# A layer-norm, attention and gated-MLP kernel: the first query pair by seven products, and final adds from PSUM

## The chip, the cores and the metric

The kernel runs on one core of one Trainium2 chip. The metric is device time in microseconds, the median of several runs. Engines: TensorE (PE, and PEld for its weight loads), VectorE (DVE), ScalarE (ACT), GpSimd (POOL) and SyncE (SP), which issues nearly all DMAs. Each engine works through its own queue in program order and waits on semaphores.

## The reference, cut to what matters

```
xn = layernorm(x)                                  # x: 1 x 2048 x 512, bf16
q  = (xn @ wq) in 32 heads of 128
p  = softmax(q k^T / sqrt(128)); o = p v           # k_cache, v_cache: 32 heads, 2048 keys
s  = concat(o) @ wo
gate = xn @ W_gate; up = xn @ W_up                 # F = 1792
y  = (gate * (gate > 0) * up) @ W_down
out = x + s * silu(y)
```

## The kernel before, in words

The 2048 rows stand in four query blocks `Q` of 512 (16 tiles of 128 rows). All is one straight program; the order on each engine is the order in which the Python code emits.

**Start.** `head_ln` centres the rows of block 0 (`xc_sb`, transposed by TensorE into `xcT`). `emit_gate_up(0)` then runs the 14 chunks `fc` of 128 columns of gate and up for block 0 from these centred rows: 4 matmuls of gate, 4 of up, a ReLU on ScalarE into `gr_sb`, and a product `h` on VectorE (L620). Behind each chunk `ln_task(fc)` does a piece of the layer norm of the other rows: `ln_stats` of one tile, and once per block `ln_sqrt` on ScalarE, then `ln_finish(Q)`: coefficients on VectorE (`ln_coef`, L400, L403), four normalised tiles `xn_sb` on GpSimd (L409), and for each a DMA transpose into `xnT` issued by SP (L521). Blocks 1, 2, 3 come in this order at chunks 4, 8 and 12; SP then issues the first loads of keys, values and weights (`issue_first`), and block 0's own normalised tiles follow at chunk 13, with the factors `r2`, `r2h` of block 0's output.

`emit_down(0)` multiplies block 0's `h` with `W_down`: four tiles `j` of 14 matmuls into two banks of `ps_acc` in turn (L747). Each tile has a tanh on ScalarE (L755), and two operations on VectorE (L759, L763) that write `g_sb`; the tile after next waits for them. `emit_gate_up(2)` is the same as above for block 2, from `xnT`; into its chunks are put the scaling of `W_down` and its sums (`emit_wd_scale`, `emit_wd_sums`), row sums of `xnT` (`emit_tx`), sums of `h` (`emit_hs`) and `gu_sums`, the weight sums of one gate/up chunk of blocks 1 and 3 (scaling on ScalarE, four operations on GpSimd).

**Products.** Most later multiplications are done as 2 x 2 blocks by seven products instead of eight (Winograd's form): sums of weights (`emit_sw` for a pair of query heads, on GpSimd, into `SW`) and sums of rows (`emit_tx`, on VectorE, into `TX`, which lies over `xn_sb` and therefore waits until all sixteen transposes have read it), and the combination of the products on VectorE. For a pair `pr` of query heads that is `emit_st(pr, c, step)`, with `c` a half of the columns and four steps of two, two, two and one products, each of two matmuls. `emit_tx(k)` with `k = 4 c + i` makes the row sum `i` of half `c`. Pair 0 alone is projected directly by `emit_qp`: eight groups of four matmuls (L815).

**Attention.** 128 blocks `b` (head x query block), each of 8 pairs `p` of key tiles. For a pair: two score matmuls (L1258), one exponential on ScalarE (L1270), eight PV matmuls of 129 columns (L1367). Scores run `LAG` = 3 pairs ahead. Scores and all side products share three slots of two PSUM banks, in turn (`ring_acquire`): a slot is free when the work that read it last has ended. `emit_M(items)` takes a slot for side products. The table `plan` sets products at a `(b, p)`, `side` sets VectorE work there. At a block's end VectorE normalises (L1287, L1290), and the first PV matmul of the next block waits for this.

**End.** `emit_base` (L1235, L1240), by the list `base_at`, makes the part of the output that does not need the last four heads, two operations on VectorE for each tile. `emit_final_tile(n)` multiplies the last four heads' output with `wo` (four matmuls, L1401), scales by `g_sb` on VectorE into `fin_tmp` (L1409) and has GpSimd add (L1425), VectorE for the last tile alone; SP stores.

Of the kernel before, what the change touches and what calls it, by code (L numbers as in the profile page):

```python
# [52 lines left out]
def bass_recurrent_scan__mha_block_cached__glu_gated_reglu__prompt_kernel(  # L53
# [62 lines left out]
    with ExitStack() as es:  # L116
# [70 lines left out]
        cu = at_(92160, [128, NQ], F32, "cu")  # L187
        cv = at_(94208, [128, NQ], F32, "cv")
# [336 lines left out]
        def ln_task(i):  # L525
            if i < 4 * (QB - 1):
                ln_hold["st"] = ln_stats(4 + i)
                if i % 4 == 3:
                    ns = list(range(i + 1, i + 5))
                    ln_hold["sq"] = (ns, ln_sqrt(ns, ln_aggr(ns, ln_hold["st"])))  # L530
                elif i >= 4 and i % 4 == 0:
                    ln_finish(i // 4)
            elif i == 4 * (QB - 1):
                ln_finish(QB - 1)
                issue_first()
                ns = list(range(4))
                ln_hold["sq"] = (ns, ln_sqrt(ns, sem_ln2.cur()))
            elif i == 4 * (QB - 1) + 1:
                ctok = ln_finish(0)
                _wait(dve, ctok)  # L540
                rtok = sem_ln3.sig(
                    dve.scalar_tensor_tensor(r2[:], rstd[:, 0:4, :], YSC, rstd[:, 0:4, :],
                                             op0=ALU.mult, op1=ALU.mult))
                _wait(dve, rtok)
                ln_hold["r2"] = sem_ln3.sig(
                    dve.tensor_scalar(r2h[:], r2[:], 0.5 / YSC, None, op0=ALU.mult))
# [38 lines left out]
        def gu_sums(k):  # L585
# [13 lines left out]
            gu_tok[(k, "x")] = sem_sg.sig(pool.tensor_tensor(X[:, 3], a12, X[:, 1], ALU.subtract))  # L599

# [133 lines left out]
        def emit_down(Q, h_last_tok):  # L734
            assert Q == 0
            ytok = None
            for j in range(4):
# [28 lines left out]
                acc_free[jb] = gtok  # L766
            y_last["t"] = ytok
# [5 lines left out]
        _wait(sp, sem_g.cur())  # L773
        gu_load(0)
        gu_load(1)
        hlast = emit_gate_up(2)

        qt_ready = {}
        qp_done_tok = {}
# [28 lines left out]
        def emit_qp(h, Q, bank):  # L808
            qs = slice(Q * NQ, (Q + 1) * NQ)
            _wait(pe, wq_tok(0))  # L810
            if h == 0 and Q == 0:
                _wait_all(pe, xt_ready[0])
            ins = None
            for c in range(DC):
                ins = pe.matmul(ps_r[:, bank, :], Wq_sb[0][:, c, h, :], xnT[:, c, qs],  # L815
                                start=(c == 0), stop=(c == DC - 1))
            qtok = sem_qp.sig(ins)
            if h == 1 and Q == QB - 1:
                qp_done_tok[0] = qtok
            dst = qt_take(h, Q)  # L820
            if h == 0 and Q % 2 == 1:
                _wait(act, qtok)
                etok = sem_gua.sig(act.copy(dst, ps_r[:, bank, :]))
            else:
                _wait(dve, qtok)
                etok = sem_qpe.sig(dve.tensor_copy(dst, ps_r[:, bank, :]))
            qt_ready[(h, Q)] = etok
            return etok

        sw_tok = {}  # L830

        def emit_sw(pr):
            b = pr % 2
            W = Wq_sb[b]
            _wait(pool, wq_tok(pr))
            if pr >= 3:
                _wait(pool, qp_done_tok[pr - 2])
            wflat = W[:].rearrange("p c i e -> p (c i e)")
            if pr == 2:
                _wait(act, wq_tok(pr))  # L840
                k = sem_w2s.sig(act.activation(wflat, wflat, ACTF.Copy, scale=WSC))
            else:
                k = sem_sw.sig(pool.tensor_scalar(wflat, wflat, WSC, None, op0=ALU.mult))  # L843
            sw_tok[(pr, 0)] = k
            _wait(pool, k)
            a11, a12 = W[:, 0:HC, 0, :], W[:, HC:DC, 0, :]
            a21, a22 = W[:, 0:HC, 1, :], W[:, HC:DC, 1, :]
            X = SW[b]
            if pr == 1:
                _wait(pool, glu_done_tok)  # L850
            k1 = sem_sw.sig(pool.tensor_tensor(X[:, 0], a21, a22, ALU.add))
            sem_sw.sig(pool.tensor_tensor(X[:, 2], a11, a21, ALU.subtract))
            _wait(pool, k1)
            k2 = sem_sw.sig(pool.tensor_tensor(X[:, 1], X[:, 0], a11, ALU.subtract))
            _wait(pool, k2)
            sw_tok[(pr, 1)] = sem_sw.sig(pool.tensor_tensor(X[:, 3], a12, X[:, 1], ALU.subtract))

        st_tok = {}

        def emit_st(pr, c, step, *banks):  # L860
            W, X = Wq_sb[pr % 2], SW[pr % 2]
# [24 lines left out]
            if step == 0:  # L886
                _wait(pe, sw_tok[(pr, 0)])
                p1 = prod(1, banks[0])
# [365 lines left out]
        def emit_S_tile(gp, tt):  # L1254
# [8 lines left out]
            if p == NP - 1:  # L1263
                qt_free.append((qt_slot[(h, Q)], stok))
                if Q == QB - 1:
# [5 lines left out]
                               scale=scale if h < 2 else scale / WSC)  # L1271
# [119 lines left out]
        def emit_final_tile(n, bank):  # L1391
# [12 lines left out]
            fb = fin_cnt[0] % NFT  # L1404
            fin_cnt[0] += 1
            _wait(dve, otok)
            _wait(dve, fin_free[fb])
            mtok = sem_opa.sig(
                dve.scalar_tensor_tensor(fin_tmp[fb], ps_r[:, bank, 0:D], 1.0 / (OSC * YSC), g_sb[:, n, :],  # L1409
                                         op0=ALU.mult, op1=ALU.mult))  # L1410
            fin_pending.append((n, fb, mtok))
            flush_final_add()
            return mtok

        fin_pending = []

        def flush_final_add():
            if not fin_pending:
                return
            n, fb, mtok = fin_pending.pop()  # L1420
            Q, j = divmod(n, 4)
            eng, sem = (dve, sem_opa) if n == NT - 1 else (pool, sem_hp)
            _wait(eng, mtok)
            _wait(eng, base_done[n])
            ftok = sem.sig(eng.tensor_tensor(g_sb[:, n, :], s_acc[:, n, :], fin_tmp[fb], ALU.add))  # L1425
            fin_free[fb] = ftok
            if Q == QB - 1 or j % 2 == 1:
                n0 = n if Q == QB - 1 else n - 1
                _wait(sp, ftok)
                sem_out.sig(sp.dma_start(out_t[:, n0:n + 1, :], g_sb[:, n0:n + 1, :]))  # L1430

# [5 lines left out]
        at(0, 0, (emit_qp, 1, 1, 0), (emit_qp, 1, 1, 1))  # L1437
        at(1, 0, (emit_qp, 1, 1, 2), (emit_qp, 1, 1, 3))
# [29 lines left out]
        for i in range(4):  # L1468
            side.setdefault((i // 2, (6, 7)[i % 2] if i < 2 else (1, 3)[i % 2]), []).append((emit_tx, i))
# [28 lines left out]
        base_at += [(LB + 1, 6), (LB + 1, 7), (LB + 2, 2), (LB + 2, 6)]  # L1498
# [7 lines left out]

# [96 lines left out]
```

## Time and profile before

| | |
|---|---|
| median of 3 runs | 1255.91 us (1255.69 to 1256.41) |
| the profiled execution | 1255.73 us, of which the span 1254.1 |
| granted TensorE clock | 1.000 |
| busy share of the span: PE, DVE, ACT, POOL | 98%, 54%, 81%, 23% |

A timeline row gives the start, the length, the engine, the line, the operation, the tile written and the tiles read, and how often; in brackets, how long the engine stood idle before it and what released it. "SPq" is SP's issuing of a DMA, not the transfer. A matmul's length is that of its way through the array; the next starts earlier. A few matmul records are missing, so a count can be one or two short. A group row of the page has the busy time, the mean in ns, and the idle time before.

### The profile page before, as it was taken

The numbers are of one execution on the slowest core, as the hardware profiler recorded it, in microseconds if no ns is written. First come the engines' busy times: TensorE is split into PE (matmuls) and PEld (weight loads), VectorE is DVE, ScalarE is ACT, GpSimd is POOL, SyncE is SP. The second block draws the span as 40 slices with busy tenths as digits, with TensorE's granted clock in tenths as the row PEclk, the third lists the DMA queues.
The fourth block names the chain that finished last, engine by engine and source line by source line (L and its number), as shares of the span: only waits on it lengthen the run. The fifth ranks groups of instructions, "written<-read, shape, count | busy, mean of one in ns | idle before, by whom it ended". The sixth has DMA issues, their size and how long they took to land.

```text
span 1254.1 us, 28671 instructions
## 1 busy us (share of the span) xinstructions
PE 1234.5 (98%) x12173; PEld 868.8 (69%) x12399; DVE 681.7 (54%) x1157; ACT 1020.3 (81%) x1108; POOL 290.3 (23%) x261
## 2 busy tenths in 40 slices
PE   9999999999999999999999999999999999999998
PEld 5466565777777777777777777777777777777774
DVE  6667777665444545454543544454544444446766
ACT  4357877668888888888888888888888888888894
POOL 2323999510401040100401040102200040100005
PEclk9999999999999999999999999999999999999999
DMA  9712431332223332443222232433333222343212
GB/s 273 155 31 31 78 79 27 51 48 34 48 44 56 69 60 47 60 68 56 52 41 44 57 56 52 60 64 60 51 56 68 50 34 42 60 81 68 67 33 76
DMA packets 250687, 78.02 MB, mean 62 GB/s; under 512 B 226241, under 2 KB 250561, under 8 KB 250561
## 3 DMA queue, kind: packets, MB, share of 16 engines
q1 hardware_dynamic: 249888, 75.79, 32.6%
q8 instruction: 98, 1.61, 0.6%
q10 hardware_dynamic: 672, 0.39, 0.1%
q14 instruction: 29, 0.23, 0.1%
HBM read 38.54 MB, written 2.10 MB: 32 GB/s over the span
## 4 chain that ended last, share of the span: by engine, by line
PE 84%; ACT 10%; POOL 2%; issue 1%; SPq 1%; DVE 1%; DMA 0%; POOLq 0%; DVEq 0%; ACTq 0%
PE ps_acc L1367 34%; PE ps_r L1258 28%; ACT PT L1270 10%; PE ps_r L1139 6%; PE ps_r L879 6%; PE ps_r L943 3%; PE ps_r L1002 3%; PE ps_r L656 1%; PE ps_r L660 1%; PE ps_r L1401 1%; PE ps_r L815 1%; POOL hT L921 0%; SPq L521 0%; POOL xn_sb L409 0%; POOL gB L919 0%
## 5 line engine op out<-in xcount | busy, mean ns | idle before, releaser
L1270 ACT ACTIVATE PT<-ps_r 128x1024 bf16<-128x1024 f32 x1024 | 969.9, 1028 | 161.2 <-PE ps_r L1258 149.7
L1367 PE MATMUL ps_acc<-V_sb,PT 128*128 128x129 bf16 x8192 | 749.2, 220 | 10.0 <-DVE Onorm L1290 1.3
L1367 PEld LDWEIGHTS ps_acc<-V_sb,PT 128*128 128x128 bf16 x8192 | 605.0, 98 | 219.0 <-ACT PT L1270 16.0
L1258 PE MATMUL ps_r<-QT_sb,KT_sb 128*128 128x512 bf16 x1831 | 652.7, 379 | 2.0 <-ACT PT L1270 0.2
L1157 DVE TENSOR_TENSOR s_acc<-s_acc,ps_r 128x512 f32<-128x512 f32 x264 | 167.7, 683 | 178.1 <-PE ps_r L1139 178.1
L843 POOL TENSOR_SCALAR Wq_sb<-Wq_sb 128x1024 bf16<-128x1024 bf16 x14 | 38.8, 2771 | 675.9 <-DMA Wq_sb<-in_A_wq_dram 675.9
L1258 PEld LDWEIGHTS ps_r<-QT_sb,KT_sb 128*128 128x128 bf16 x2048 | 188.0, 98 | 1.6 <-ACT PT L1270 0.7
L1287 DVE RECIPROCAL rz_sb<-ps_acc 128x4 f32<-128x4 f32 x127 | 23.2, 183 | 204.1 <-PE ps_acc L1367 203.8
L1290 DVE TENSOR_TENSOR Onorm<-ps_acc,rz_sb 128x512 bf16<-128x512 f32 x127 | 87.8, 691 | 4.4
L884 DVE TENSOR_TENSOR QT_sb<-cu,ps_r 128x512 bf16<-128x512 f32 x60 | 41.3, 688 | 84.6 <-PE ps_r L1258 79.5
L1425 POOL TENSOR_TENSOR g_sb<-s_acc,WX 128x512 bf16<-128x512 f32 x15 | 17.8, 1216 | 153.9 <-DVE WX L1409 153.9
L879 PE MATMUL ps_r<-xn_sb,SW 128*128 128x512 f16 x180 | 48.6, 379 | 0.0
L1139 PE MATMUL ps_r<-WX,OX 128*128 128x256 f16 x336 | 45.8, 273 | 0.0
L884 DVE TENSOR_TENSOR cu<-cu,ps_r 128x512 f32<-128x512 f32 x60 | 41.3, 688 | 0.0
L1139 PEld LDWEIGHTS ps_r<-WX,OX 128*128 128x128 f16 x336 | 32.9, 98 | 9.8 <-ACT PT L1270 0.2
L884 DVE TENSOR_TENSOR QT_sb<-cv,ps_r 128x512 bf16<-128x512 f32 x60 | 38.3, 680 | 0.0
L1081 POOL TENSOR_SCALAR Wo_sb<-Wo_sb 128x2048 bf16<-128x2048 bf16 x7 | 37.6, 5366 | 0.6
L879 PEld LDWEIGHTS ps_r<-xn_sb,SW 128*128 128x128 f16 x180 | 17.6, 98 | 21.3 <-ACT PT L1270 0.3
L879 PE MATMUL ps_r<-xnT,Wq_sb 128*128 128x512 bf16 x120 | 30.8, 379 | 0.0
L1139 PE MATMUL ps_r<-Wo_sb,OT_store 128*128 128x256 bf16 x224 | 29.0, 273 | 0.4
L616 ACT ACTIVATE gr_sb<-ps_r 128x512 bf16<-128x512 f32 x27 | 15.7, 593 | 16.7 <-PE ps_r L656 16.0
L919 POOL TENSOR_SCALAR gB<-gB 128x512 bf16<-128x512 bf16 x14 | 20.8, 1487 | 32.2 <-DVE gB L949 32.2
(151 smaller groups left out, 942.4 us busy)
## 6 DMA issues: line engine op xcount, KB each, us to landing
V_sb<-in_A_v_cache_dram SPq DMA_DIRECT2D x32, 512.0 KB, 4.8
Wq_sb<-in_A_wq_dram SPq DMA_DIRECT2D x16, 256.0 KB, 3.8
Wo_sb<-in_A_wo_dram SPq DMA_DIRECT2D x8, 512.0 KB, 3.8
xr_sb<-in_A_x_dram SPq DMA_DIRECT2D x16, 128.0 KB, 2.1
OT_store<-Onorm SPq DMA_TRANSPOSE x127, 2.5
Wd_sb<-in_B_W_down_dram SPq DMA_DIRECT2D x1, 1792.0 KB, 14.0
W<-in_B_W_gate_dram SPq DMA_DIRECT2D x14, 128.0 KB, 2.5
W<-in_B_W_up_dram SPq DMA_DIRECT2D x14, 128.0 KB, 2.8
```

Source lines behind the costliest of these rows:

```text
L843: k = sem_sw.sig(pool.tensor_scalar(wflat, wflat, WSC, None, op0=ALU.mult))
L879: ins = pe.matmul(ps_r[:, bank, :], L(i), R(i), start=(i == 0), stop=(i == HC - 1))
L884: return sem_qpe.sig(dve.tensor_tensor(dst, a, ps_r[:, bank, :], op))
L943: ins = pe.matmul(ps_r[:, bank, :], L(i), R(i), start=(i == 0), stop=(i == HC - 1))
L1002: ins = pe.matmul(ps_r[:, bank, j * DH:(j + 1) * DH], L(i), R(i), start=(i == 0 and j == 0), stop=(i == HF - 1 and j == 1))
L1081: k = sem_wx.sig(pool.tensor_scalar(wflat, wflat, WOSC, None, op0=ALU.mult))
L1139: ins = pe.matmul(ps_r[:, bank, j * DH:(j + 1) * DH], L(i), R(i), start=(i == 0 and j == 0), stop=(i == GH - 1 and j == 1))
L1157: t = dve.tensor_tensor(names[k], names[k], view(bank), op)
L1258: ins = pe.matmul(ps_r[:, 2 * s + tt, :], KT_sb[h % 2][:, t * 128:(t + 1) * 128], QT_sb[qt_slot[(h, Q)]][:], start=True, stop=True)
L1270: act.activation(PT[pb][:], ps_r[:, 2 * s:2 * s + 2, :], ACTF.Exp, scale=scale if h < 2 else scale / WSC)
L1290: dve.tensor_tensor(Onorm[ob][:], o_ap, rz_sb[:].to_broadcast([128, 4, Dh]), ALU.mult))
L1367: ins = pe.matmul(o_ap, PT[pb][:, tt, j * 128:(j + 1) * 128], V_sb[vb][:, t, 0:VW], start=(t == 0 and j % 2 == 0), stop=(t == KT - 1 and j ...
```

## The change

- Block 0's normalised rows come first: the square root at chunk 1, `ln_finish(0)`, `r2` and `r2h` at chunk 2 of the first gate/up.
- The eight row sums `emit_tx` move into `emit_down`, two behind each tile's `g_sb`.
- Pair 0 goes by seven products: `emit_sw(0)` (scaling on ScalarE) behind chunk 0 of `emit_gate_up(2)`, the steps of the first half behind chunks 9 to 12, step 0 of the second half behind chunk 13, and its other three in attention blocks 0 and 1. `gu_sums` moves from chunks 4 and 6 to 7 and 9, `emit_hs` from 10 and 11 to 12 and 13. The combinations of the first half use buffers of their own (`cuv0`, `SW0`).
- The first three score pairs (`emit_S_pair`) stand behind chunks 12 and 13 instead of after them.
- Tiles 0 to 7, 10, 13 and 15 of the end are scaled in place in PSUM and added by VectorE; the others stay with GpSimd.
- The last four entries of `base_at` move to later pairs.

```diff
@@ ln_task
+                if i == 1:
+                    ns = list(range(4))
+                    ln_hold["sq"] = (ns, ln_sqrt(ns, sem_ln2.cur()))
                 ln_hold["st"] = ln_stats(4 + i)
+                if i == 2:
+                    ctok = ln_finish(0)
...
@@ emit_sw
-            if pr == 2:
+            if pr in (0, 2):
                 _wait(act, wq_tok(pr))
...
@@ emit_gate_up, Q == 2
-                    elif fc < 10:
-                        emit_tx(fc - 2)
-                    elif fc < 12:
-                        emit_hs(2, 0, 2 * (fc - 10))
-                        emit_hs(2, 0, 2 * (fc - 10) + 1)
-                    if fc in (4, 6):
-                        gu_sums(fc // 2 - 2)
+                    if fc == 0:
+                        emit_sw(0)
+                    if fc in (7, 9):
+                        gu_sums((fc - 7) // 2)
+                    if 9 <= fc < 12:
+                        emit_M([(emit_st, 2, 0, 0, fc - 9)])
+                    elif fc == 12:
+                        emit_S_pair(0)
+                        emit_M([(emit_st, 1, 0, 0, 3)])
+                    elif fc == 13:
+                        emit_S_pair(1)
+                        emit_M([(emit_st, 2, 0, 1, 0)])
+                        emit_S_pair(2)
+                    if fc > 11:
+                        emit_hs(2, 0, 2 * (fc - 12))
+                        emit_hs(2, 0, 2 * (fc - 12) + 1)
@@ emit_down, end of tile j
                 acc_free[jb] = gtok
+                emit_tx(2 * j)
+                emit_tx(2 * j + 1)
@@ emit_final_tile
+            sums_on_dve = n < NT - 8 or n in (NT - 6, NT - 3, NT - 1)
...
+            if sums_on_dve:
+                eng, sem, prod = dve, sem_opa, ps_r[:, bank, 0:D]
+            else:
+                eng, sem = pool, sem_hp
...
@@ plan and main
-        at(0, 0, (emit_qp, 1, 1, 0), (emit_qp, 1, 1, 1))
-        at(1, 0, (emit_qp, 1, 1, 2), (emit_qp, 1, 1, 3))
+        for step, b, p in ((1, 0, 0), (2, 1, 0), (3, 1, 3)):
+            at(b, p, (emit_st, 1 if step == 3 else 2, 0, 1, step))
...
-        base_at += [(LB + 1, 6), (LB + 1, 7), (LB + 2, 2), (LB + 2, 6)]
+        base_at += [(LB + 2, 2), (LB + 2, 5), (LB + 3, 1), (LB + 3, 3)]
...
-        for Q in range(0, QB, 2):
-            emit_M([(emit_qp, 1, 0, Q), (emit_qp, 1, 0, Q + 1)])
         sp_head_start(0)
-        for gp in range(LAG):
-            open_S_pair(gp)
-            emit_S_tile(gp, 0)
-            emit_S_tile(gp, 1)
         emit_sw(1)
```

`LB` is 124, the first block of the last head.

More of the change, by code (lines that the diff above doesn't have):

```diff
@@ L535, in ln_task @@
                 issue_first()
[L536 to L546, printed above, removed]
         HS = S // 2
@@ L806, in qt_take @@
             return QT_sb[i][:]
[L808 to L838, printed above, removed]
-            if pr == 2:
[L840 to L856, printed above, removed]
         st_tok = {}
         def emit_st(pr, c, step, *banks):
-            W, X = Wq_sb[pr % 2], SW[pr % 2]
+            W, X = Wq_sb[pr % 2], SW[pr % 2] if pr else SW0
+            cu, cv = cuv0 if pr == 0 and c == 0 else cuv
             lo = slice(c * NQ, (c + 1) * NQ)
@@ L887, in emit_st @@
                 _wait(pe, sw_tok[(pr, 0)])
+                if pr == 0 and c == 0:
+                    _wait_all(pe, xt_ready[0])
                 p1 = prod(1, banks[0])
@@ L1505, in bass_recurrent_scan__mha_block_cached__glu_gated_reglu__prompt_kernel, with emit_S_pair @@
                 plan[(LB + 2 + Q, 4 * (j // 2))][-1].append((emit_final_tile, 1, 4 * Q + j))
+        def emit_S_pair(gp):
+            open_S_pair(gp)
+            emit_S_tile(gp, 0)
+            emit_S_tile(gp, 1)
+        assert LAG == 3 and FC == 14
+        _wait(sp, sem_g.cur())
+        gu_load(0)
+        gu_load(1)
+        hlast = emit_gate_up(2)
         glu_done_tok = hlast
```

78 lines of the change are left out of this document (50 added, 28 removed).

## The prediction

> **What bounds the kernel now.** I read the page first: the span, the busy shares, the clock row and the shares of the chain.
>
> ```profile
> span 1254.1 us, 28671 instructions
> PE 1234.5 (98%) x12173; PEld 868.8 (69%) x12399; DVE 681.7 (54%) x1157; ACT 1020.3 (81%) x1108; POOL 290.3 (23%) x261
> PEclk9999999999999999999999999999999999999999
> PE 84%; ACT 10%; POOL 2%; issue 1%; SPq 1%; DVE 1%; DMA 0%; POOLq 0%; DVEq 0%; ACTq 0%
> ```
>
> TensorE (PE) is busy 98% of the span at the full clock, so every matmul removed counts whole, and otherwise only the 2% where PE stands still can be won. The change touches two places, so I read PE's timeline there: the stretch from the first down product to the first PV matmul, and the last blocks.
>
> ```profile
> 31.24 12.25 PE L747 MATMUL ps_acc<-Wd_sb,hT 128*128 128x512 bf16 x54
> 57.65 1.02 PE L656 MATMUL ps_r<-xnT,Wg_sb 128*128 128x512 bf16 x4 [0.34 <-DVE hT L620]
> 68.00 3.79 PE L815 MATMUL ps_r<-xnT,Wq_sb 128*128 128x512 bf16 x16
> 73.40 0.61 PE L1258 MATMUL ps_r<-QT_sb,KT_sb 128*128 128x512 bf16 x2 [0.25 <-ACT PT L1270]
> 74.31 1.90 PE L815 MATMUL ps_r<-xnT,Wq_sb 128*128 128x512 bf16 x8 [0.31 <-ACT PT L1270]
> 76.05 1.06 PE L1367 MATMUL ps_acc<-V_sb,PT 128*128 128x129 bf16 x12
> ```
>
> The eight matmuls of 512 columns at 74.31 are followed by PV at 76.05: 0.217 us each, or 0.216 over longer runs. From 31.24 to 76.05 the code issues 200 such matmuls (56 down, 112 gate/up, 24 projection, 8 score): 43.2 us of 44.8. So **1.6 us** of waiting lie there: VectorE late behind the weight scaling at 57, then the empty pipeline at 72 to 74, where three score pairs wait for the first exponentials. At the end:
>
> ```profile
> 1219.83 0.69 DVE L1205 TENSOR_TENSOR s_acc<-s_acc 128x512 f32<-128x512 f32 x1
> 1221.28 0.69 DVE L1235 SCALAR_TENSOR_TENSOR s_acc<-s_acc,g_sb 128x512 f32<-128x512 f32 x1
> 1223.34 0.69 DVE L1240 TENSOR_TENSOR s_acc<-s_acc,xr_sb 128x512 f32<-128x512 f32 x1
> 1223.94 0.18 DVE L1287 RECIPROCAL rz_sb<-ps_acc 128x4 f32<-128x4 f32 x1
> 1224.16 0.69 DVE L1290 TENSOR_TENSOR Onorm<-ps_acc,rz_sb 128x512 bf16<-128x512 f32 x1
> 1221.85 1.89 PE L1401 MATMUL ps_r<-Wo_sb,OT_store 128*128 128x512 bf16 x8
> 1224.99 0.61 PE L1367 MATMUL ps_acc<-V_sb,PT 128*128 128x129 bf16 x8 [1.25 <-DVE Onorm L1290]
> ```
>
> VectorE runs two base pairs (four operations from 1221.28) before the reciprocal. PE has issued its eight final-tile matmuls by 1221.85 + 8 x 0.216 = 1223.58 and resumes at 1224.99: **1.41 us** lost, the largest single wait after the start.
>
> **The change, part by part.**
>
> *Seven products.* Eight projections of four matmuls become 2 x 7 x 2 = 28 matmuls: 4 x 0.216 = **-0.86 us** on PE. The added combinations on VectorE, 16 where 6 casts stood, go beside gate/up matmuls; their price is this row's 688 ns:
>
> ```profile
> L884 DVE TENSOR_TENSOR cu<-cu,ps_r 128x512 f32<-128x512 f32 x60 | 41.3, 688 | 0.0
> ```
>
> From chunk 9 on a chunk has 8 x 0.216 = 1.73 us of gate/up and 0.86 of products; VectorE has 0.69 for `h` and at most 3 x 0.69. It keeps up except at two ring slots: chunk 13 follows step 2's three combinations, which end some 0.2 us after PE could start; and step 1 of the second half (plan (0,0)) needs the slot of step 0, whose two combinations stand behind `h` of chunk 13: about 0.5 us. **+0.64 us** for both, nothing to 0.9. In return the **1.6 us** of old waits go: the weight scaling of `gu_sums` moves from chunk 4 to 7, when its load has long landed (the block-0 transposes no longer stand before it on SP's queue), and the exponentials of pairs 0 to 2 run beside chunk 13.
>
> *Block 0's norm early, row sums in the first down.* This is what costs. On VectorE the coefficients and `r2` (six small operations, about 1.2 us) go between chunks 2 and 3 of the first gate/up. Each chunk there leaves about 0.5 us (1.73 less 2 x 0.6), a slot is asked for three chunks later, so the delay is gone before PE sees it: 0. But `emit_tx(0)` now stands on VectorE right behind the first `g_sb` tile, and waits for all sixteen transposes of `xn_sb`. Queued behind it are `emit_tx(1)` and both operations of tile 1, and PE's fourth down tile waits for these, since it reuses their bank.
>
> ```profile
> 13.74 0.69 DVE L383 BATCH_NORM_STATS2 stats<-x_sb 128x6 f32<-128x512 bf16 x1
> 18.63 3.04 POOL L409 TENSOR_SCALAR xn_sb<-x_sb,rstd,nmr 128x512 bf16<-128x512 bf16 x4 [16.95 <-DVE nmr L403]
> L521 SPq DMA_TRANSPOSE xnT<-xn_sb x4: 1267/1621/2092, 19.4 to 24.9; - x4
> 19.43 18.17 SPq L521 DMA_TRANSPOSE xnT<-xn_sb  x12
> 31.68 6.28 POOL L409 TENSOR_SCALAR xn_sb<-x_sb,rstd,nmr 128x512 bf16<-128x512 bf16 x8 [3.28 <-DVE nmr L403]
> L521 SPq DMA_TRANSPOSE xnT<-xn_sb x2: 1264/1264/1265, 35.0 to 36.3; - x2
> DMA to landing us min/median/max: 2.5/2.5/2.5
> ```
>
> Now the last of block 3 is issued at 36.3 and lands 2.5 later, L = 38.8, SP issuing back to back from the first one at 19.43. The change puts four more in front. Block 0's coefficients follow the statistics of 13.74 (0.6 to the next operation, 0.4 for coefficients, 0.76 for a norm): its first transpose can start at 15.5. Sixteen back to back then end as follows. Lower bound: at 1.27 + 0.04 each they would be done by 36.5, so block 3's norms from 31.68 still bind, L = 38.8. Upper bound: eight at the longest 2.09 + 0.04 and eight at 1.31 end at 43.0; the last starts 1.3 earlier: L = 44.2. At the mean of the twelve, 18.17 / 12 = 1.51, they end at 39.7: L = 40.9; with the first six at 1.69 (the four from 19.4 average 1.65 and a gap, while the weights still load) and the rest at 1.31, at 38.7: L = 40.0. I take **L = 40.3**, by these four, the nearest rows.
>
> ```profile
> 59.07 0.68 DVE L562 TENSOR_TENSOR xn_sb<-xnT 128x1024 f16<-128x1024 bf16 x1
> 59.67 0.68 DVE L620 TENSOR_TENSOR hT<-gr_sb,ps_r 128x512 f16<-128x512 bf16 x1
> 60.27 1.18 DVE L564 TENSOR_TENSOR xn_sb<-xnT 128x1024 f16<-128x1024 bf16 x1
> 60.24 0.66 POOL L594 TENSOR_TENSOR SG<-W 128x256 f16<-128x256 bf16 x1
> 38.20 0.49 DVE L759 TENSOR_SCALAR sig_sb<-sig_sb,r 128x512 f32<-128x512 f32 x1 [1.67 <-ACT sig_sb L755]
> 38.73 0.69 DVE L763 TENSOR_TENSOR g_sb<-sig_sb,ps_acc 128x512 bf16<-128x512 f32 x1
> 45.97 1.08 DVE L683 TENSOR_SCALAR Wd_sb<-Wd_sb 128x3584 bf16<-128x3584 bf16 x1
> ```
>
> GpSimd is idle then, so a row sum takes 0.68, not 1.18, and the next operation starts 0.6 after it (59.07, 59.67). Behind L come two row sums 1.22, then 0.52 + 0.69 for tile 1, and 0.17 until PE starts: L + 2.6. PE would start that tile at 31.24 + 42 x 0.216 = 40.3. Wait: **+2.6 us** (+1.1 at L = 38.8, +6.5 at 44.2). VectorE then reaches `h` of gate/up chunk 0 some 1.4 us late; chunk 3 asks for that slot 1.1 us after it is free, since scaling and `h` (1.08 + 0.61) just fit a chunk of 1.73: nothing on PE.
>
> There the four sums of `emit_sw(0)` on GpSimd are new. Row and neighbour show such a meeting: L564 waited until L594 had ended at 60.90 and took 1.18. Each of four can cost VectorE 0.5 so; 2.0 against 1.1 of slack: 0 to +0.9, I take 0. [...]
>
> *Base pairs later.* The two pairs leave VectorE before the reciprocal; PV's last matmul goes two score tiles (0.43) before 1221.85 and has ended by 1221.65, so the norm is ready by 1222.7, before 1223.58: **-1.41 us**. The pairs go into blocks 126 and 127, where GpSimd no longer adds.
>
> *Final adds.* Tiles 0 to 7 hold their bank for four operations, 2.7 us, where PE asks again after 2.2 us plus the 0.5 that the first tile is ahead: even, 0 to +0.3. In the tail:
>
> ```profile
> 1245.39 0.69 DVE L1409 SCALAR_TENSOR_TENSOR WX<-ps_r,g_sb 128x512 bf16<-128x512 f32 x1 [0.23 <-POOL g_sb L1425]
> 1246.48 0.69 DVE L1409 SCALAR_TENSOR_TENSOR WX<-ps_r,g_sb 128x512 bf16<-128x512 f32 x1 [0.40 <-PE ps_r L1401]
> 1249.93 0.69 DVE L1409 SCALAR_TENSOR_TENSOR WX<-ps_r,g_sb 128x512 bf16<-128x512 f32 x1 [0.17 <-PE ps_r L1401]
> 1250.66 1.65 DVE L1425 TENSOR_TENSOR g_sb<-s_acc,WX 128x512 bf16<-128x512 f32 x1
> 1246.16 5.60 POOL L1425 TENSOR_TENSOR g_sb<-s_acc,WX 128x512 bf16<-128x512 f32 x5 [0.77 <-DVE WX L1409]
> ```
>
> The last add takes 1.65 beside GpSimd's; from PSUM I price it by L884's 0.69: -0.96. But tile 10's add holds its bank to 1246.8, and tiles 12 and 13 take that bank: PE, ready at 1246.49, loses 0.45 with the hand-over. Tile 13's add puts VectorE back another 0.2, and tile 14's store on SP (after GpSimd's 1.15) stands before the last one, 0.4. Together **+0.1 us** (-0.5 to +0.4).
>
> **Sum:** -0.86 - 1.6 + 0.64 + 2.6 - 1.41 + 0.1 = **-0.5 us**. The profiled execution took 1255.73, its span 1254.1 and 1.6 around it, 0.2 under the median of the runs, 1255.91. Off that median: **1255.4 us**.
>
> **The rivals.**
>
> *SP keeps pace.* If issues take 1.27 whatever is loading, L stays at 38.8: -2.0, 1253.9; if the two ring waits vanish too, 1253.3. For it: most issues in the rows are 1.26 to 1.28. Against: the four at 19.4.
>
> *SP falls behind and the fourth down tile waits for it* (the slower side). The first eight issues go at the pace of the loads, up to 2.09 each. The time passes +0.2% when L passes 43.3; at 44.2 it is 1255.4 + 3.9 = 1259.3. For it: slow issues stand exactly where weights load, and the change puts four more there. Against: only one of four took 2.09.
>
> *PE's clock drops in the wait.* This takes a wait that is long enough, and none in this trace is: the 1.41 us gap above stands in full clock.
>
> ```profile
> 1221.00:1225.00 4.00, 2.70 (x18) 1.22 (x17) 3.86 (x8) 2.40 (x3) 0.00 (x0) 1.00 0.00 0
> ```
>
> If the wait of the down tile were more than twice that and the tile's 14 matmuls then ran at half pace, they would add 14 x 0.216 = 3.0 us; at L = 41.5, 1255.4 + 1.2 + 3.0 = 1259.6. [...]
>
> *The base pairs do not free the norm* (the change not doing what it says): other work on VectorE comes before the reciprocal. No row speaks for it; 1255.4 + 1.4 = 1256.8.
>
> **How the numbers follow.** Forecast (L 39.3 to 41): 0.53. SP keeps pace: 0.26, in three of four of these beyond the bound, with the smaller waits gone as well. SP falls behind: 0.08. Clock: 0.08. Base pairs: 0.05. A measurement of this kernel can tell about 0.2%, 2.5 us, from no change: faster is below 1253.4, slower above 1258.4. Faster 0.20, slower 0.16, the rest 0.64. The range goes from the best of the first rival, 1253.2, to 1257.9: L at 41.8 and 0.9 for the lock.
>
> **What would show it.** Right: a PE idle of 2 to 3 us before the fourth group of down matmuls, released by VectorE, with the first row sum starting at about 40; no PE idle at 57; PV's first matmul near 77; the 1.25 before L1367 at the end gone; the last add at 0.7. Wrong: the down wait under 1.2 (first rival) or over 4, a clock under 1.00 in the 43 to 47 window, or a new PE idle in gate/up chunks 3 to 8.

## The result and the profile after

| | before | after |
|---|---|---|
| median | 1255.91 us | 1261.72 us (1261.27 to 1262.66, 6 runs) |
| span of the profiled execution | 1254.1 | 1260.5 |

The ratio is 1.0046 (95% interval 1.0033 to 1.0059): slower by 5.8 us, above the predicted 1255.4 and above the range's end of 1257.9. The page's head of the changed kernel:

```profile
span 1260.5 us, 28901 instructions
PE 1247.9 (99%) x12395; PEld 869.0 (69%) x12395; DVE 690.1 (55%) x1177; ACT 1020.4 (81%) x1107; POOL 280.0 (22%) x255
PEclk9899999999999999999999999999999999999999
```

The busy share rose from 98 to 99% and says nothing: before, 226 more matmul records are missing (12173 of 12399, of which the change takes four). What is new is the 8 in the second slice of the clock row, 31 to 63 us. PE's timeline there, and VectorE's:

```profile
35.64 4.91 PE L787 MATMUL ps_acc<-Wd_sb,hT 128*128 128x512 bf16 x22
46.15 5.95 PE L787 MATMUL ps_acc<-Wd_sb,hT 128*128 128x512 bf16 x14 [5.60 <-DVE g_sb L803]
51.94 0.38 PE L687 MATMUL ps_r<-xnT,Wg_sb 128*128 128x512 bf16 x1
```

```profile
43.68 0.69 DVE L564 TENSOR_TENSOR xn_sb<-xnT 128x1024 f16<-128x1024 bf16 x1 [7.21 <-DMA xnT<-xn_sb]
44.29 0.68 DVE L566 TENSOR_TENSOR xn_sb<-xnT 128x1024 f16<-128x1024 bf16 x1
44.89 0.48 DVE L799 TENSOR_SCALAR sig_sb<-sig_sb,r 128x512 f32<-128x512 f32 x1
45.41 0.69 DVE L803 TENSOR_TENSOR g_sb<-sig_sb,ps_acc 128x512 bf16<-128x512 f32 x1
```

The fourth down tile waits, as predicted, for tile 1's `g_sb`, which stands behind the first two row sums, which wait for a transpose. But the transpose lands at 43.56, not at 40.3, and the tile's 14 matmuls then take 51.94 - 46.15 = 5.79 us, 0.41 each, not 0.216. The view by stretches has the granted clock in the column behind the engines:

```profile
40.00:46.00 6.00, 0.55 (x3) 0.06 (x1) 2.28 (x4) 0.69 (x1) 0.00 (x0) 0.91 0.69 150
46.00:52.00 6.00, 5.85 (x15) 2.15 (x16) 3.68 (x7) 0.00 (x0) 0.00 (x0) 0.52 1.27 246
```

At half clock a stretch shows 0.50, so PE had it for 0.09 x 2 x 6 + 0.48 x 2 x 6 = 6.8 us, from about 44.9 to 51.8. The first 1.2 us of that fell into the wait; the 14 matmuls lost 5.79 - 14 x 0.216 = 2.8 us. The second gate/up begins at 51.94 instead of 43.33: 8.6 us later. Why the transpose lands late stands in SP's issues (the instructions of tile `xnT`, then those of line 320; the second row of each is from issue to landing):

```profile
L522 SPq DMA_TRANSPOSE xnT<-xn_sb x16: 1264/1265/5811, 15.7 to 41.1; - x16
DMA to landing us min/median/max: 2.5/2.7/10.8
```

```profile
L320 SPq DMA_DIRECT2D Wd_sb<-in_B_W_down_dram x1: 1419/1419/1419, 12.0 to 12.0; - x1
DMA to landing us min/median/max: 13.9/13.9/13.9
```

Block 0's first transpose is issued at 15.7, as early as predicted, and lands 10.8 us later, at 26.5. `W_down`, issued at 12.0 just ahead of it, lands at 25.9. The trace of before holds the same, in a view that the prediction read for another stretch (the last two columns are the share of the DMA engines and GB/s; the last line is for the twelve transposes that the prediction counts):

```profile
21.00:24.00 3.00, 2.95 (x15) 1.36 (x14) 1.97 (x7) 1.11 (x3) 0.66 (x1) 1.00 1.10 346
24.00:26.00 2.00, 2.00 (x11) 0.87 (x9) 1.97 (x6) 0.86 (x2) 0.63 (x1) 1.00 1.59 123
```

```profile
DMA to landing us min/median/max: 2.4/3.2/7.1
```

The DMA engines were full (a share of 1.10, 346 GB/s) until 24, and before, too, the first transpose (19.4) landed 7.1 us after its issue, at 26.5. The issue 3.7 us earlier gained nothing on that landing. Nor did SP get ahead with the next ones. The first two issues, after and then before:

```profile
L522 SPq DMA_TRANSPOSE xnT<-xn_sb x2: 1371/3591/5811, 15.7 to 21.6; - x2
L521 SPq DMA_TRANSPOSE xnT<-xn_sb x2: 1365/1728/2092, 19.4 to 21.6; - x2
```

The issue at 15.7 itself took 5.81 us, and the second went at 21.6 in both kernels. The rest of the change went mostly as forecast. The seven products, the scores and the first blocks, PE and then VectorE:

```profile
78.01 1.02 PE L687 MATMUL ps_r<-xnT,Wg_sb 128*128 128x512 bf16 x4
82.34 1.04 PE L867 MATMUL ps_r<-xn_sb,SW 128*128 128x512 f16 x4 [0.28 <-DVE QT_sb L872]
83.21 0.62 PE L1357 MATMUL ps_acc<-V_sb,PT 128*128 128x129 bf16 x8
85.80 1.38 PE L992 MATMUL ps_r<-Wd_sb,hT 128*128 128x256 bf16 x11 [0.66 <-DVE cuv L872]
```

```profile
82.20 1.08 DVE L764 TENSOR_TENSOR HS_sb<-hT 128x1024 f16<-128x1024 f16 x1
83.31 1.04 DVE L767 TENSOR_TENSOR HS_sb<-hT,HS_sb 128x1024 f16<-128x1024 f16 x1
84.28 1.47 DVE L872 TENSOR_TENSOR cuv<-cuv,ps_r 128x512 f32<-128x512 f32 x2
```

From the second gate/up to PV it takes 83.21 - 51.94 = 31.27 us, before 32.72. The wait at 85.80 is new: the first down product needs the ring slot of step 1, whose combinations start late behind two down sums of 1.08 and 1.04. At the end (PE at block 126, PE in the tail, VectorE's last add):

```profile
1229.41 1.89 PE L1392 MATMUL ps_r<-Wo_sb,OT_store 128*128 128x512 bf16 x8
1231.14 0.62 PE L1357 MATMUL ps_acc<-V_sb,PT 128*128 128x129 bf16 x8
```

```profile
1253.03 3.19 PE L1392 MATMUL ps_r<-Wo_sb,OT_store 128*128 128x512 bf16 x14 [0.43 <-DVE g_sb L1410]
```

```profile
1257.63 0.69 DVE L1410 TENSOR_TENSOR g_sb<-ps_r,s_acc 128x512 bf16<-128x512 f32 x1
```

Eight matmuls after 1229.41 PV follows at once (1229.41 + 1.73): the 1.41 us are gone. In the tail PE stops for 0.6 us before 1253.03 (four matmuls after 1251.57 would end at 1252.44), until tile 10's add frees its bank. The last add takes 0.69.

### The profile page after: what moved, and what is told of

Same layout as the page of the kernel before. It is cut to its first block, busy times and chain, and to the rows that moved or that the text cites. A ratio compares the mean times of both kernels' runs of the same rounds, so it can differ in the third digit from the quotient of the medians.

```text
span 1260.5 us, 28901 instructions
## 1 busy us (share of the span) xinstructions
PE 1247.9 (99%) x12395; PEld 869.0 (69%) x12395; DVE 690.1 (55%) x1177; ACT 1020.4 (81%) x1107; POOL 280.0 (22%) x255
## 3 DMA queue, kind: packets, MB, share of 16 engines
q8 instruction: 98, 1.61, 0.6%
## 4 chain that ended last, share of the span: by engine, by line
PE 95%; POOL 2%; DVE 1%; SPq 0%; DMA 0%; issue 0%; ACT 0%; DVEq 0%; POOLq 0%; ACTq 0%
PE ps_acc L1357 36%; PE ps_r L1248 34%; PE ps_r L867 7%; PE ps_r L1129 7%; PE ps_r L933 3%; PE ps_r L992 3%; PE ps_r L687 2%; PE ps_r L691 2%; PE ps_r L1392 1%; SPq L522 0%; PE ps_acc L787 0%; POOL hT L911 0%; POOL xn_sb L410 0%; POOL gB L909 0%; POOL gA L909 0%
## 5 line engine op out<-in xcount | busy, mean ns | idle before, releaser
L1248 PE MATMUL ps_r<-QT_sb,KT_sb 128*128 128x512 bf16 x2048 | 726.8, 379 | 0.0
L872 DVE TENSOR_TENSOR QT_sb<-cuv,ps_r 128x512 bf16<-128x512 f32 x128 | 84.9, 684 | 85.6 <-PE ps_r L1248 79.5
L872 DVE TENSOR_TENSOR cuv<-cuv,ps_r 128x512 f32<-128x512 f32 x96 | 66.0, 688 | 3.3
L867 PE MATMUL ps_r<-xn_sb,SW 128*128 128x512 f16 x192 | 51.9, 379 | 0.3 <-DVE QT_sb L872 0.3
L1412 POOL TENSOR_TENSOR g_sb<-s_acc,WX 128x512 bf16<-128x512 f32 x5 | 5.7, 1156 | 164.4 <-DVE WX L1405 164.4
L647 ACT ACTIVATE gr_sb<-ps_r 128x512 bf16<-128x512 f32 x27 | 15.7, 594 | 19.3 <-PE ps_r L687 18.7
L1129 PEld LDWEIGHTS ps_r<-Wo_sb,OT_store 128*128 128x128 bf16 x224 | 21.9, 98 | 8.5
```

The costliest lines, as they stand in the source:

```text
L867: ins = pe.matmul(ps_r[:, bank, :], L(i), R(i), start=(i == 0), stop=(i == HC - 1))
L872: return sem_qpe.sig(dve.tensor_tensor(dst, a, ps_r[:, bank, :], op))
L1129: ins = pe.matmul(ps_r[:, bank, j * DH:(j + 1) * DH], L(i), R(i), start=(i == 0 and j == 0), stop=(i == GH - 1 and j == 1))
L1248: ins = pe.matmul(ps_r[:, 2 * s + tt, :], KT_sb[h % 2][:, t * 128:(t + 1) * 128], QT_sb[qt_slot[(h, Q)]][:], start=True, stop=True)
```

## The experiments

Each run has its own runs of the kernel before beside it (medians 1255.77 to 1256.54); ratios are to those, with 95% intervals. What is not marked otherwise is changed in the changed kernel. "Wait" is PE's idle time before the fourth down tile.

| run | median, us | ratio | interval |
|---|---|---|---|
| e1_rows_late | 1259.05 | 1.0023 | 1.0014 to 1.0033 |
| e2_fill30 | 1261.05 | 1.0038 | 1.0025 to 1.0051 |
| e3_wd_behind | 1260.12 | 1.0033 | 1.0021 to 1.0044 |
| e4_base_only | 1254.40 | 0.9988 | 0.9979 to 0.9998 |
| e6_fill48 | 1259.64 | 1.0030 | 1.0018 to 1.0041 |
| e7_wd_act | 1260.98 | 1.0042 | 1.0027 to 1.0057 |
| e8_spread | 1255.19 | 0.9996 | 0.9987 to 1.0006 |
| e9_spread_sw1 | 1255.11 | 0.9994 | 0.9984 to 1.0003 |
| e10_sw1_held | 1254.28 | 0.9989 | 0.9980 to 0.9998 |
| e11_direct_early | 1252.91 | 0.9976 | 0.9967 to 0.9986 |
| e12_half_wd | 1258.64 | 1.0023 | 1.0014 to 1.0032 |
| e13_adds_no10 | 1252.25 | 0.9965 | 0.9952 to 0.9979 |

**What holds the transposes.** First, `W_down` behind block 0's transposes:

```diff
-        sem_wd.sig(sp.dma_start(Wd_sb[:], ...))      # with the loads of the start
+                    # in ln_task, directly behind ln_finish(0) and its four transposes
+                    sem_wd.sig(sp.dma_start(Wd_sb[:], ...))
```

> The changed kernel with one DMA moved on SP: the load of W_down (1.8 MB) is issued behind block 0's four transposes instead of before them. Theory (SP's first transpose is held until 21.5 because its queue is full of the loads before it, mostly W_down): the first transpose issues in under 3 us, the last of block 3 lands near 39.3 instead of 43.6, PE waits 1.3 to 2 us before the fourth down tile at full clock: 1261.7 - 4.3 - 2.95 = about 1254.5 us. Rival (the first transpose of a kernel takes long by itself, or is held by any load under way): it still ends near 21.5, last landing 43 or later, 1261 us or more.

SP's issues:

```profile
15.80 5.21 SPq L521 DMA_TRANSPOSE xnT<-xn_sb  x4
21.05 0.58 SPq L533 DMA_DIRECT2D Wd_sb<-in_B_W_down_dram  x1
21.68 19.38 SPq L521 DMA_TRANSPOSE xnT<-xn_sb  x12
```

Block 0's four go at 1.30 each, with x and gate/up weights still loading. The next three, right behind `W_down`, take 2.66, 2.30 and 1.75, and the last of the sixteen lands at 42.28. The delay moved with the load and cost 1.3 us less; the time is far from the expected (1260.12 against 1254.5), for the wait is still 4.22 us and the clock still falls, to 0.50 between 46 and 48. Next, the same load on another queue:

```diff
-        sem_wd.sig(sp.dma_start(Wd_sb[:], ...))
+            if i == 0:                                # ln_task
+                sem_wd.sig(act.dma_start(Wd_sb[:], ...))
```

> The changed kernel with the load of W_down issued on ScalarE's queue (at the end of the first gate/up chunk, about 14 us) instead of on SP's, the same bytes at nearly the same time. Theory (a transpose's issue is held by a load that stands ahead of it on its own queue): the sixteen transposes go at 1.27 to 1.31 each, the last lands at 38.8 to 39.5, the fourth down tile waits 1.1 to 1.8 us at the full clock, and the time is 1261.72 - 4.3 - 2.95 = 1254.5 us. Rival (any large load under way holds them): last landing near 43.5, 1261.7 us. ScalarE issues the load between relus and may lose up to 1.4 us to that.

```profile
L521 SPq DMA_TRANSPOSE xnT<-xn_sb x16: 1264/1268/2899, 15.6 to 40.3; - x16
DMA to landing us min/median/max: 2.5/3.0/11.2
```

The theory of SP's queue falls. ScalarE issued the load at 10.0, earlier than expected, and it landed at 26.5; SP now got four transposes out by 25.5, at 2.1 to 2.9 us each, but the first still landed 11.2 us after its issue, at 26.8. The last lands at 42.78, and the time is 1260.98. What counts should then be the bytes ahead:

```diff
-        sem_wd.sig(sp.dma_start(Wd_sb[:], ...))
+        sem_wd.sig(sp.dma_start(Wd_sb[:, 0:FC // 2, :], wd_src[:, 0:FC // 2, :]))
+                # behind block 3's transposes
+                sem_wd2.sig(sp.dma_start(Wd_sb[:, FC // 2:FC, :], wd_src[:, FC // 2:FC, :]))
-                                    Wd_sb[:, fc, :], ...
+                                    Wd_sb[:, fc % (FC // 2), :], ...
```

> The changed kernel with only the first half of W_down loaded ahead of the transposes (7 of 14 row blocks, 0.9 MB less) and the second half behind them; the first down product uses the first half twice, so the gate of block 0 is not the reference's. Theory (the transposes cannot move until the loads ahead of them, which fill the DMA engines at about 350 GB/s, are through; SP runs only some four ahead): 0.92 MB / 0.35 MB per us = 2.6 us earlier, first landing at 23.9, the last at 41.0, a wait of 3.2 us before the fourth down tile with one window of 3.41 us at half clock, 1261.72 - 2.6 - 1.2 = 1257.9 us. Rival (the first transposes take long whatever is loading): landings near 26.5 and 43.5 as before, 1261.7 us.

```profile
L524 SPq DMA_TRANSPOSE xnT<-xn_sb x16: 1264/1265/3279, 15.8 to 39.0; - x16
DMA to landing us min/median/max: 2.5/2.5/8.2
```

```profile
44.05 5.88 PE L792 MATMUL ps_acc<-Wd_sb,hT 128*128 128x512 bf16 x14 [3.38 <-DVE g_sb L808]
```

It is so: `W_down`'s half lands at 23.4 and the first transpose at 24.0 (15.8 + 8.2), 2.5 us earlier than after; the last lands at 41.45, and the wait is 3.38. The time is 1258.64, 0.7 over the expectation. In the profiled execution, 1259.64, the clock stayed at half for 6.8 us and not 3.4. That is not the median's account: three of the ten executions took 1259.64 to 1260.07 with a mean granted clock of 0.997, the other seven 1258.27 to 1258.67 with 0.998 or 0.999. What makes up the median's 0.7 is not shown.

**What the standing still costs.** PE got matmuls to do in the wait:

```diff
                     pe.wait_ge(sem_wd.h, 16)
+                if j == 3:
+                    warm_mm(30)                       # 48 in the second run
```

> The changed kernel with 30 useless matmuls of 256 columns put before the fourth down tile's wait, into a PSUM bank that is free then: 3.2 us of the idle time are filled, 2.4 remain. The wait ends when it did. Theory (an idle stretch of 5.6 us halves the clock, one of 2.4 does not): the 14 matmuls behind it go at 0.216, 1261.7 - 2.95 = about 1258.8 us, clock 1.000. Rival (the slow matmuls come from the transfers of keys and values that run at that time): 14 matmuls at 0.427 again, 1261.7 us.

> The changed kernel with 48 matmuls of 256 columns whose result nobody reads (48 x 0.108 = 5.2 us) on PE before the fourth down tile, so that PE stands still for at most about 1 us where the tile waits for the row sums. 30 of them had left 3.35 us of standing still and the clock still fell. Theory (the clock falls because PE stands still): the clock stays at 1.00 through the fourth down tile, its 14 matmuls go at 0.216, and the time is 1261.72 - 2.95 = 1258.8 us. Rival (the clock falls there for another reason): 1261.7 us.

Thirty were too few: 3.18 us of waiting remained by the bracket (2.9 in fact: the record of the tile's first matmul is missing, and `g_sb` is written by 46.55), the clock went to half for 3.4 us, and the time hardly moved. One of the five executions came out at the 1258.8 that the theory gives, 1258.78 with a mean granted clock of 1.000, the other four at 1261.02 to 1261.20 with 0.998; only one of the four left a trace. With 48:

```profile
40.48 5.54 PE L440 MATMUL ps_r<-const-bfloat16-1.0 128*128 128x256 bf16 x48
47.63 2.97 PE L789 MATMUL ps_acc<-Wd_sb,hT 128*128 128x512 bf16 x13 [1.61 <-DVE g_sb L805]
```

```profile
48.00:50.00 2.00, 2.00 (x11) 0.88 (x9) 1.97 (x4) 0.00 (x0) 0.00 (x0) 1.00 1.25 258
```

the clock holds (1.00 in the second fence, the view by stretches) and the tile runs at 0.216; here, too, the first matmul's record is missing, and the wait is 1.4 us, not 1.61. PE does 5 us more of useless work and the kernel is 2.1 us faster by the medians, 1.6 by the profiled executions (1260.23 against 1261.81). In this one the last transpose landed at 44.81, 1.25 us later than after; 1.6 + 1.25 is the 2.8 that the slow clock had cost.

**The row sums elsewhere.** First two behind each of the chunks 6 to 9 of the second gate/up, then one behind each of 2 to 9 with `emit_sw(0)` at chunk 4:

```diff
-                emit_tx(2 * j)                        # emit_down
-                emit_tx(2 * j + 1)
+                    if 6 <= fc < 10:                  # e1_rows_late
+                        emit_tx(2 * (fc - 6))
+                        emit_tx(2 * (fc - 6) + 1)
+                    if 2 <= fc < 10:                  # e8_spread
+                        emit_tx(fc - 2)
-                    if fc == 0:
+                    if fc == 4:                       # e8_spread
                         emit_sw(0)
```

> The changed kernel with its eight row sums back in the second gate/up, two behind each of chunks 6 to 9; all else as changed. Theory: the loss is the wait of the fourth down tile for the row sums (PE idle 5.8 us) and the half-pace clock after it (14 matmuls at 0.427 in place of 0.216, 2.95 us). Both go: 1261.7 - 5.8 - 2.95 = about 1253.0 us, clock 1.000, no PE step over 1 us between 31 and 60. Rival (the loss comes from the seven products and their combinations on VectorE): still 1259 us or more.

> The changed kernel with the eight row sums taken out of the first down product and put one behind each of the chunks 2 to 9 of the second gate/up, and emit_sw(0) moved from chunk 0 to chunk 4, when its load has landed, so that no relu stands behind a wait for it. Theory (the loss is the down wait and the slow clock behind it, and the misses of the earlier run with late row sums came from the relu held by emit_sw(0) and from two row sums per chunk): no wait before the fourth down tile, clock 1.00, no wait at the seven products: 1261.72 - 5.6 - 2.95 = 1253.2 us. Rival (GpSimd's sums beside the row sums hold VectorE late whatever the order): waits of 1 to 3 us at the ring slots of chunks 8 to 10, 1255 to 1256 us.

In both the fourth down tile waits for nothing. In the first, other waits came instead, ScalarE's, VectorE's and PE's:

```profile
48.28 1.06 ACT L615 ACTIVATE Wq_sb<-Wq_sb 128x1024 bf16<-128x1024 bf16 x1 [3.22 <-DMA Wq_sb<-in_A_wq_dram]
```

```profile
49.92 0.69 DVE L651 TENSOR_TENSOR hT<-gr_sb,ps_r 128x512 f16<-128x512 bf16 x1 [2.79 <-ACT gr_sb L647]
```

```profile
67.41 1.44 PE L868 MATMUL ps_r<-xn_sb,SW 128*128 128x512 f16 x4 [2.57 <-DVE xn_sb L572]
```

Chunk 1's relu stood on ScalarE behind the scaling of `Wq`, whose load SP issues only behind the sixteen transposes, so VectorE began 2.8 us late. It never made that up, since some row sums took 1.04 to 1.18 beside GpSimd's sums, and step 1, which needs them all, waited 2.57 us; the clock then fell for 3.4 us (0.50 between 68 and 70). (Three of its ten executions, 1256.96 to 1257.64, show a mean granted clock of 1.000, the others 0.999 or 0.998.) Moved as in e8_spread, the relu is free and the clock whole (0.999 to 1.000), and 1255.19 is 6.5 us better than the changed kernel. It still misses 1253.2, by four waits that add up to 1.8 us from matmul to matmul (0.43, 0.31, 0.58, 0.44); three have a bracket:

```profile
59.50 1.02 PE L687 MATMUL ps_r<-xnT,Wg_sb 128*128 128x512 bf16 x4 [0.27 <-DVE hT L651]
64.70 1.02 PE L867 MATMUL ps_r<-xn_sb,SW 128*128 128x512 f16 x4 [0.41 <-DVE xn_sb L572]
66.01 1.04 PE L687 MATMUL ps_r<-xnT,Wg_sb 128*128 128x512 bf16 x3 [0.28 <-DVE QT_sb L872]
```

The time is the rival's (1255 to 1256), though its single waits of 1 to 3 us did not come. Two causes meet in the trace, and no run separates them: in chunks 2 to 5 VectorE has `h`, a sum of `W_down` and a row sum, 0.6 + 1.0 + 0.6 = 2.2 us of work in a chunk of 1.73, and four of the eight row sums take 1.15 to 1.18 us beside GpSimd's sums in place of 0.68.

**The wait at 85.80.** Two tries to keep GpSimd's `emit_sw(1)` away from VectorE's down sums, both on top of e8_spread:

```diff
-        emit_sw(1)                                    # behind the last chunk
+                emit_sw(1)                            # block 0, step 4: e9 and e10
                 gu_sums(2)
-                _wait(pool, glu_done_tok)             # e10 alone
+                _wait(pool, hs_tok[(2, 1, 3)])
```

> As e8_spread, and emit_sw(1) moved from behind the last chunk to block 0, step 4 of the main loop, so that GpSimd's sums for the second pair do not run beside the first down sums of VectorE (emit_hs 2 and 3, 1.04 and 1.08 us instead of 0.69). Theory: the wait of 0.7 to 0.8 us at the main loop's first seven-product step goes, 1253.2 - 0.8 = 1252.4 us. Rival (the wait there has another cause, or the sums meet other VectorE work in block 0): no difference from e8_spread.

> As e8_spread, and GpSimd's sums of emit_sw(1) wait for the last of the four down sums of VectorE that run in block 0 (emit_hs(2, 1, 3)); moving the call alone, as in e9_spread_sw1, had left them at the same time, since nothing else stood before them on GpSimd. Theory (these sums make emit_hs 2 and 3 take 1.08 and 1.04 us instead of 0.69, and so step 1's combinations late): both take 0.68 to 0.69, the 0.66 us before the first down product goes to 0.1 or less, and the time is 0.7 to 0.8 us under e8_spread's 1255.19: 1254.4 us. Rival (the wait has another cause): both sums shorten or not, the wait stays, 1255.2 us.

e9_spread_sw1 tested nothing: with no work between, GpSimd ran the sums at the same time as before the move, from 74.53 (74.16 in e8_spread), and the time is 1255.11. Held by a wait, they run from 83.92, behind the down sums:

```profile
75.89 0.69 DVE L766 TENSOR_TENSOR HS_sb<-hT 128x1024 f16<-128x1024 f16 x1
76.61 0.69 DVE L769 TENSOR_TENSOR HS_sb<-hT,HS_sb 128x1024 f16<-128x1024 f16 x1
```

1.08 and 1.04 become 0.69, PE no longer waits there, and the time is 0.9 us lower, 1254.28 (0.7 when each is set against the kernel before beside it): the theory holds.

**The parts that gain, alone.** The moved base pairs in the kernel before, then with early direct projections and score tiles, then with the change's final adds but tile 10's on GpSimd:

```diff
# e4_base_only, e11, e13
-        base_at += [(LB + 1, 6), (LB + 1, 7), (LB + 2, 2), (LB + 2, 6)]
+        base_at += [(LB + 2, 2), (LB + 2, 5), (LB + 3, 1), (LB + 3, 3)]
# e11_direct_early, e13: second gate/up
-                    if fc in (4, 6):
-                        gu_sums(fc // 2 - 2)
+                    if fc in (7, 9):
+                        gu_sums((fc - 7) // 2)
+                    if fc in (10, 12):
+                        emit_M([(emit_qp, 1, 0, fc - 10), (emit_qp, 1, 0, fc - 9)])
+                    if fc > 10:
+                        emit_S_pair(fc - 11)
...                                                   # their old calls behind the last chunk go
# e13_adds_no10: the changed kernel's emit_final_tile with
+            sums_on_dve = n < NT - 8 or n in (NT - 3, NT - 1)
```

> The kernel before with one part of the change alone: the last four base pairs at their later places. Theory: the 1.41 us that PE lost before the first PV matmul of block 126 goes, 1255.9 - 1.4 = 1254.5 us. Rival (the four operations only turn up as another wait in blocks 126 and 127, where GpSimd still adds): 1255.9 us.

> The kernel before with three things of the change alone: the last base pairs in blocks 126 and 127; gu_sums behind chunks 7 and 9; and the projections of head 0 and the score tiles of pairs 0 to 2 between the last chunks of the second gate/up, but as direct projections (four matmuls each), with the row sums, the norm of block 0 and its transposes where they were. Theory (the gains of the change are the 1.41 us before block 126's norm and the 1.6 us of waits between the first down product and PV; its losses all come from the row sums in the first down product and from VectorE's combinations): 1255.96 - 1.41 - 1.6 = 1252.95 us, nothing lost at the ring. Rival (work between the chunks makes VectorE or ScalarE late at the ring there as well, as in e8_spread, about 1.5 us): 1254.4 us, as with the base pairs alone.

> e11_direct_early with the change's final adds, but tile 10's add left on GpSimd (tiles 0 to 7, 13 and 15 are added from PSUM on VectorE). In the changed kernel the stretch from the last block's first PV matmul to the end of the span is 18.83 us, before 18.58, with 0.6 us of it lost on PE where tile 12's matmuls wait for tile 10's bank. Theory (that 0.6 is tile 10's add, and the last add's shortening from 1.65 to 0.69 counts as far as tile 14's store lets it): no such wait, stretch 18.83 - 0.6 = 18.2 us, time 1252.91 - 0.35 = 1252.6 us. Rival (the hand-over of the last tiles costs the same without tile 10's add): stretch 18.8 us, 1253.2 us.

All three come out as the theories say, to 0.1, 0.1 and 0.4 us: 1254.40, 1252.91 and 1252.25. In e11_direct_early PE runs from the first down product to PV nearly without a stop:

```profile
31.35 12.25 PE L751 MATMUL ps_acc<-Wd_sb,hT 128*128 128x512 bf16 x56
72.92 1.89 PE L815 MATMUL ps_r<-xnT,Wq_sb 128*128 128x512 bf16 x8
74.64 0.62 PE L1367 MATMUL ps_acc<-V_sb,PT 128*128 128x129 bf16 x8
```

43.29 us, before 44.81. In e13_adds_no10 the matmuls of tiles 11 to 15 follow each other without the wait of 1253.03 (19 in one row), the stretch from the last block's first PV matmul to the end is 1251.0 - 1232.79 = 18.2 us as expected (18.6 before, 18.8 after), and the last add takes 0.69. It is the fastest kernel of the case, 0.35% under the kernel before, though it projects pair 0 directly, as before. How much of that the final adds give is known less well: the kernel before took 1256.54 beside this run and 1255.77 beside e11_direct_early, while the spans of the two profiled executions, 1251.0 and 1251.3, differ by the 0.3 to 0.4 of the theory.

```profile
1232.79 0.62 PE L1367 MATMUL ps_acc<-V_sb,PT 128*128 128x129 bf16 x8
1242.90 4.26 PE L1402 MATMUL ps_r<-Wo_sb,OT_store 128*128 128x512 bf16 x19
```

## Why the prediction was wrong

The chain was right and two of its terms were not.

- **L, the landing of the last block-3 transpose: 43.56 against 40.3.** PE starts the fourth tile at 46.15, L + 2.59, the forecast step; so the wait of 5.8 us is the 2.6 plus the 3.3 by which L was wrong, less 0.1 by which PE came later. The step that failed is "sixteen back to back from 15.5", priced "by these four, the nearest rows", that is by the issues of before at 19.4. It took 26.65 us where about 23.6 were forecast. An issue's length of 1.27 to 2.09 there is that of transposes issued 3 to 7 us before they landed. The one issued at 15.7 stood behind `W_down`, landed 10.8 us later, and its issue took 5.81 us, more than the longest row that the bounds allowed for; the second went at 21.6, as before. So nothing was won by the early start, and the four added transposes cost nearly what they take: 4 x 1.31 = 5.2 us, less 0.5 since the slow issue just ahead of block 3's took 2.20 before and one took 1.73 after. Half of `W_down` behind them gave 2.1 us of L back. L itself lay inside the bounds (44.2), as the rival "SP falls behind" had it: the choice between the ends was wrong, and the row that would have decided it is the landing of the first transpose, 7.1 us after its issue.
- **The clock: +2.8, not in the sum.** It was a rival at 0.08, priced at L = 41.5, and "SP falls behind" another at 0.08, above 43.3. No row or run gives 41.5 as a limit; the traces show the clock falling at L = 41.45 (e12_half_wd), 42.28 (e3_wd_behind), 42.78 (e7_wd_act) and 43.56 (after). The two were told as alternatives, but the second contains the first: past L = 43.3 the forecast's own wait is 5.6, and with 5.60 the clock fell, so that at 43.6 the prediction's own prices give 1255.4 + 3.3 + 3.0 = 1261.7, not the 1258.7 that its rival gave alone. (That this meets the measured 1261.72 is in part luck, since the next term is not in it.) Nor was a wait "more than twice" the 1.41 us needed: in e1_rows_late the clock fell after 2.57 us, so the forecast's own 2.6 at the full clock was not safe.
- **The wait of the first down product for step 1's slot: +0.8, not foreseen.** The prediction weighed GpSimd's sums of pair 0 against VectorE's work and took 0 rightly; those of pair 1 met VectorE in the same way where no chunk of gate/up stood between to make up for it. Beside them the two down sums took 1.08 and 1.04 us, apart from them 0.69 each (e10_sw1_held). The 0.9 "for the lock" in the prediction's range is its upper estimate, four times 0.5 less 1.1 of slack; no run shows a lock, only the longer times.
- **Right:** the waits at 57 and 72 to 74 are gone and the two ring slots cost 0.17 + 0.45 = 0.62 (forecast 0.64): from the second gate/up to PV -1.45, by -1.6 - 0.43 (two matmuls fewer up to there) + 0.62. The base pairs gave their 1.41 (e4_base_only: 1.5). The last add shrank to 0.69 and tile 10's bank cost 0.6 (0.45); the tail is 0.25 longer (0.1).

Forecast -0.5, plus 3.2, 2.8, 0.8 and 0.15, is about +6.4; the spans of the profiled executions differ by 6.4, their times by 6.1, and the medians by 5.8.

That the seven products themselves pay is not shown. They save 0.86 us of PE. The best form of them that ran, e10_sw1_held (1254.28, with the row sums among the gate/up chunks), is 1.4 us behind direct projections in the same place, e11_direct_early; how much of that belongs to the combinations, to the row sums and to the tail of the change was not separated.

## What to carry to other kernels

When an operation is moved forward, look at when its kind lands, not at how long its issue takes: here an issue 3.7 us earlier, into full DMA engines (a share of 1.10), landed at the same 26.5, and the issue behind it went at the same 21.6. In six traces a wait on TensorE of 2.57 us or more had a second price, the clock at half for 3.4 or 6.8 us; such a price belongs into the same rival as the wait, not beside it. A move in program order did not move work in time on an engine that had nothing else to do (GpSimd's sums from 74.53 in e9_spread_sw1, from 74.16 in e8_spread); a wait did (83.92, e10_sw1_held).

## What was not expected of the hardware

**The clock fell after waits of 2.6 us and more, and stayed down for 3.4 or 6.8 us.** PE's idle time by its bracket, and how long the clock was at half in the view by stretches: 1.25 (block 126, before) and 1.61 (e6_fill48, 1.4 with the missing record): none; 2.57 (e1_rows_late, with 0.81 some 4 us ahead of it) and 3.18 (e2_fill30, 2.9 with the missing record): 3.4 us; 3.38 (e12_half_wd): 6.8; 4.22 (e3_wd_behind): 3.4; 4.96 (e7_wd_act) and 5.60 (after): 6.8. So neither the length of the wait nor its end alone sets the loss: after a wait of 3.38 us the clock was at half for longer than after one of 4.22. For e3_wd_behind, half clock from about 45.4 to 48.8, beginning after PE had started again at 44.88:

```profile
44.00:46.00 2.00, 1.12 (x4) 0.46 (x5) 1.93 (x4) 0.00 (x0) 0.00 (x0) 0.85 0.97 234
46.00:48.00 2.00, 2.00 (x6) 0.76 (x5) 1.97 (x5) 0.00 (x0) 0.00 (x0) 0.50 1.32 248
48.00:50.00 2.00, 1.95 (x8) 0.79 (x7) 0.47 (x1) 0.20 (x1) 0.00 (x0) 0.80 1.38 225
```

The table has, for the six traces with a fall, its moment, PE's idle time in the 3.4 us that end there, and that in the 3.4 us that follow.

| run | fall at, us | idle in the 3.4 us before | idle in the 3.4 us after | half clock, us |
|---|---|---|---|---|
| e12_half_wd | 42.7 | 2.0 | 1.4 | 6.8 |
| e7_wd_act | 42.6 | 2.2 | 2.7 | 6.8 |
| after | 44.9 | 3.4 | 1.2 | 6.8 |
| e1_rows_late | 67.9 | 2.6 | at most 0.2 | 3.4 |
| e2_fill30 | 46.8 | 2.9 | 0 | 3.4 |
| e3_wd_behind | 45.4 | 2.9 | 0 | 3.4 |

The clock fell with 2.0 to 3.4 us idle in the 3.4 us before; before and e6_fill48, whose clock held, had waits of 1.25 and 1.4. It stayed down for 6.8 us where 1.2 to 2.7 us of the next 3.4 were idle, and for 3.4 us where at most 0.2 were. What the clock goes by is not shown. Executions of e1_rows_late and e2_fill30 differ in their mean clock (0.998 to 1.000), and those of e12_half_wd (0.997 to 0.999); no run was made to settle why.

**Another queue for the load did not help the transposes.** With `W_down` issued by ScalarE or by SP the first one landed the same 11 us after its issue (11.2 and 10.8). SP's issue was held in both, in one piece of 5.81 us behind its own load, in four of 2.1 to 2.9 us behind ScalarE's, and the fifth transpose went at 25.5 and 26.2. What holds the issue was not tested.
